# MLP gelu as one ScalarE activation from PSUM, and its second layernorm on VectorE

## The chip, the cores and the metric

The kernel runs on one core of a Trainium2 chip. Its engines are TensorE (PE, with its weight loads shown apart as PEld), VectorE (DVE), ScalarE (ACT), GpSimd (POOL) and SyncE (SP), which here issues the DMAs. The metric is the device time of one execution in microseconds, and of several runs the median.

## What is computed

Two layers, an attention (A) and a gated MLP (B), each run twice over a sequence of 2048 positions with 512 features:

```python
def _gelu(x):
    return jax.nn.gelu(x, approximate=True)

def _layernorm(x, axis=-1, eps=1e-05):
    m = jnp.mean(x, axis=axis, keepdims=True)
    v = jnp.var(x, axis=axis, keepdims=True)
    return (x - m) / jnp.sqrt(v + eps)

def _B_ref(x, w_in, w_sp, b_sp, w_out):
    z = _gelu(jnp.einsum('bsd,df->bsf', x, w_in))
    z1 = z[..., :Fh].copy()
    z2 = _layernorm(z[..., Fh:], axis=-1)
    g = jnp.einsum('ts,bsf->btf', w_sp, z2) + b_sp[None, :, None]
    return jnp.einsum('bsf,fd->bsd', z1 * g, w_out)

x = x + _A_ref(_layernorm(x, axis=-1), A_wq, A_wk, A_wv, A_wo)
x = x + _B_ref(_layernorm(x, axis=-1), B_w_in, B_w_sp, B_b_sp, B_w_out)
x = x + _A_ref(_layernorm(x, axis=-1), A_wq, A_wk, A_wv, A_wo)
x = x + _B_ref(_layernorm(x, axis=-1), B_w_in, B_w_sp, B_b_sp, B_w_out)
```

The attention has 32 query heads of 16 features and one key and value head. In the MLP w_in has 512 x 1792 values and Fh is 896.

## The kernel before

Every operation is put on its engine's program by `K.op(engine, function, waits, inc)`. An engine runs its program in the order in which it was written, and each operation waits for the semaphores in its list. So the order of the calls in the Python is the order on each engine, and only the semaphores tie engines together.

**Prologue.** SP issues the loads of x, of the attention's weights (semaphore `wA`) and of w_in and w_out (semaphore `wB`, lines 212 and 213). VectorE then spreads the attention's weights into padded tiles (L225 to L239), multiplies w_out by 0.5 (L243, which waits for `wB`), and sets up the value tile V_aug (two memsets; the last one is `w_prep`, for which PE and the loads of w_sp wait). Behind these on VectorE stand the statistics of the first layernorm (L277, L278).

**Layer A.** Scores by TensorE (L756), the exponential on ScalarE from PSUM into bf16 (L775), the product with the values by TensorE (L795), and its sum on VectorE (L816 to L820), in a pipeline that runs over 4 query chunks, 8 head groups and 16 key tiles. Side tasks, among them the projection of the queries, the output projection (L717) and in layer 0 the transposes of w_sp, are slipped in between.

**Layer B, gelu stage.** After a layernorm with transposes (L277 to L311) come 60 items: first 32 "z2" items (16 row tiles by 2 halves of 448 columns, matmuls at L904), then 28 "z1" items (4 column chunks by 7 feature tiles, 512 columns, matmuls at L909). Each item is four accumulating matmuls into one of four PSUM banks (`NSLOT = 4`). The gelu of an item is made of five steps:

- `step_pe`: the four matmuls; waits until step d4 of the item four before has freed the bank.
- `step_a0` (L942, ScalarE): a scaled square of the PSUM tile into `ybuf` (fp32).
- `step_d3` (L951, VectorE): (square + c) times the PSUM tile, in `ybuf`.
- `step_a1` (L962, ScalarE): tanh of `ybuf` into `thbuf` (bf16).
- `step_d4` (L972, VectorE): (tanh + 1) times the PSUM tile, into `z2n` or `z1c` (bf16). This is twice the gelu. The factor is made up for by the 0.5 in w_out, and by 4 times the epsilon in the second layernorm.

A loop over the items staggers the steps (`LAG`, one item apart each). A z2 item also has its statistics on VectorE (`bn_stats` L977, and for a whole tile `bn_aggr` L980), then 1/sqrt on GpSimd (L981, L983). Six items later `emit_norm` puts the second layernorm: minus mean over deviation on VectorE (L992, one column), then scale and bias of the 896-wide tile on ScalarE, in place (L995).

**Layer B, behind it.** The spatial matmul (L1060) of 16 matmuls for each of 4 chunks by 7 feature tiles. Its first group waits for the end of the gelu stage and, matmul by matmul, for each tile's norm (`vz2n`). VectorE adds the bias and multiplies by z1 (L1070, L1076), and the output projection follows (L1092, with `w_out_r`), added to X at L1098.

Of the kernel before, what the change touches and what calls it, by code (L numbers as in the profile page):

```python
# [104 lines left out]
def bass_interleave_layers__grouped_kv_mqa__mixer_gmlp__prompt_kernel(  # L105
# [52 lines left out]
    def bank32(b, n=1):  # L158
        return ps32[:, 512 * b:512 * (b + n)]
# [35 lines left out]
    with ExitStack() as wst:  # L195
# [23 lines left out]
        def dve_memset(ap, val, waits=()):  # L219
# [20 lines left out]
                wv_rep[:].rearrange("p kd (g r) -> p kd g r", r=32)[:, :, :, 0:DH],  # L240
                wv_nat[:, :, None, :].to_broadcast([P, KD, 4, DH])),
            waits=[(S_dve, v0), wA], inc=S_dve)
        K.op("dve", lambda e: e.tensor_scalar(w_out_r[:], w_out_r[:], 0.5, None, op0=ALU.mult),  # L243
             waits=[wB], inc=S_dve)
        v0 = dve_memset(V_aug[:], 0.0)
        w_prep_v = dve_memset(V_aug[:].rearrange("p t (c r) -> p t c r", r=32)[:, :, :, DH], 1.0,
                              waits=[(S_dve, v0)])
# [615 lines left out]
    def layer_B(layer_idx, x_waits):  # L863
# [12 lines left out]
        z2n = K.sb([P, NT, FH], BF16, lst, name="z2n")  # L876
        z1c = K.sb([P, NF1, S], BF16, lst, name="z1c")
        NSLOT = 4
        ybuf = K.sb([P, NSLOT, 512], FP32, lst, name="ybuf")
        thbuf = K.sb([P, NSLOT, 512], BF16, lst, name="thbuf")  # L880
        st2 = K.sb([P, NT, 2, 6], FP32, lst, name="st2")
        mv2 = K.sb([P, NT, 2], FP32, lst, name="mv2")
        veps2 = K.sb([P, NT], FP32, lst, name="veps2")
        rstd2 = K.sb([P, NT], FP32, lst, name="rstd2")
        nb2 = K.sb([P, NT], FP32, lst, name="nb2")

        items = []
        for t in range(NT):
# [28 lines left out]
            _, tc, ft = it  # L917
            return z1c[:, ft, tc * TCW:(tc + 1) * TCW]

        st = {"pe": [None] * NIT, "a0": [None] * NIT, "d3": [None] * NIT, "a1": [None] * NIT, "d4": [None] * NIT}  # L920
        vm = [None] * NT

        def step_pe(k):
            it = items[k]
            slot = k % NSLOT
            bk = bank32(slot)
            wl = [xnT_all, wB]
            if k >= NSLOT:
                assert st["d4"][k - NSLOT] is not None
                wl.append((S_dve, st["d4"][k - NSLOT]))  # L930
            st["pe"][k] = K.op("pe", lambda e, it=it, bk=bk: pe_item(e, it, bk), waits=wl, inc=S_pe)

        def step_a0(k):
            it = items[k]
            slot = k % NSLOT
            bk = bank32(slot)
            n = item_N(it)
            wl = [(S_pe, st["pe"][k])]
            if k >= NSLOT:
                wl.append((S_dve, st["d3"][k - NSLOT]))  # L940
                wl.append((S_act, st["a1"][k - NSLOT]))
            st["a0"][k] = K.op("act", lambda e, slot=slot, bk=bk, n=n: e.activation(  # L942
                ybuf[:, slot, 0:n], bk[:, 0:n], ACTF.Square, scale=SQA), waits=wl, inc=S_act)

        def step_d3(k):
            it = items[k]
            slot = k % NSLOT
            bk = bank32(slot)
            n = item_N(it)
            wl = [(S_act, st["a0"][k])]  # L950
            st["d3"][k] = K.op("dve", lambda e, slot=slot, bk=bk, n=n: e.scalar_tensor_tensor(  # L951
                ybuf[:, slot, 0:n], ybuf[:, slot, 0:n], GELU_C, bk[:, 0:n], op0=ALU.add, op1=ALU.mult),
                waits=wl, inc=S_dve)

        def step_a1(k):
            it = items[k]
            slot = k % NSLOT
            n = item_N(it)
            wl = [(S_dve, st["d3"][k])]
            if k >= NSLOT:  # L960
                wl.append((S_dve, st["d4"][k - NSLOT]))
            st["a1"][k] = K.op("act", lambda e, slot=slot, n=n: e.activation(  # L962
                thbuf[:, slot, 0:n], ybuf[:, slot, 0:n], ACTF.Tanh), waits=wl, inc=S_act)

        def step_d4(k):
            it = items[k]
            slot = k % NSLOT
            bk = bank32(slot)
            n = item_N(it)
            wl = [(S_act, st["a1"][k])]  # L970
            oap = out_ap(it)
            st["d4"][k] = K.op("dve", lambda e, slot=slot, bk=bk, n=n, oap=oap: e.scalar_tensor_tensor(  # L972
                oap, thbuf[:, slot, 0:n], 1.0, bk[:, 0:n], op0=ALU.add, op1=ALU.mult),
                waits=wl, inc=S_dve)
            if it[0] == "z2":
                _, t, h = it
                v1 = K.op("dve", lambda e, t=t, h=h: e.bn_stats(st2[:, t, h, :], z2n[:, t, h * 448:(h + 1) * 448]),  # L977
                          waits=[(S_dve, st["d4"][k])], inc=(S_dloc if h == 1 else None))
                if h == 1:
                    vm[t] = K.op("dve", lambda e, t=t: e.bn_aggr(mv2[:, t, :], st2[:, t, :, :]), waits=[(S_dloc, v1)], inc=S_dve)  # L980
                    vp1 = K.op("pool", lambda e, t=t: e.tensor_scalar(veps2[:, t:t + 1], mv2[:, t, 1:2], 4.0 * LN_EPS, None,  # L981
                                                                       op0=ALU.add), waits=[(S_dve, vm[t])], inc=S_ploc)
                    vr2[t] = K.op("pool", lambda e, t=t: e.tensor_tensor(rstd2[:, t:t + 1], veps2[:, t:t + 1], mhalf[:, 0:1], ALU.pow),  # L983
                                  waits=[(S_ploc, vp1)], inc=S_pool)
                    pending_norm.append((k + 6, t))
# [3 lines left out]
        pending_norm = []  # L989

        def emit_norm(t):
            vnb = K.op("dve", lambda e, t=t: e.scalar_tensor_tensor(nb2[:, t:t + 1], mv2[:, t, 0:1], -1.0, rstd2[:, t:t + 1],  # L992
                                                                  op0=ALU.mult, op1=ALU.mult),
                       waits=[(S_pool, vr2[t])], inc=S_dve)
            vz2n[t] = K.op("act", lambda e, t=t: e.activation(z2n[:, t, :], z2n[:, t, :], ACTF.Identity,  # L995
                                                              bias=nb2[:, t:t + 1], scale=rstd2[:, t:t + 1]),
                            waits=[(S_dve, vnb)], inc=S_act)

        LAG = [0, 1, 2, 3, 4]
        for it_k in range(NIT + 5):  # L1000
            k = it_k
            while pending_norm and pending_norm[0][0] <= k:
                emit_norm(pending_norm.pop(0)[1])
            if 0 <= k - LAG[4] < NIT:
                step_d4(k - LAG[4])
            if 0 <= k - LAG[3] < NIT:
                step_a1(k - LAG[3])
            if 0 <= k - LAG[2] < NIT:
                step_d3(k - LAG[2])
            if 0 <= k - LAG[1] < NIT:  # L1010
                step_a0(k - LAG[1])
            if k - LAG[0] < NIT and k - LAG[0] >= 0:
                step_pe(k - LAG[0])
        gelu_done = (S_dve, st["d4"][NIT - 1])
        z1_ready = gelu_done

        while pending_norm:
            emit_norm(pending_norm.pop(0)[1])
        z2n_all = (S_act, max(vz2n))

        wspT = K.sb([P, 2, NT, TCW], BF16, lst, name="wspT")
        hT2 = K.sb([P, NF1, TCW], BF16, lst, name="hT2")
# [13 lines left out]
        for tc in range(NTC):  # L1036
# [9 lines left out]
            for ft in range(NF1):  # L1046
                gb = ft % 3
                bk = bank32(2 + gb)
                wl = [z2n_all, wspT_ready, gelu_done]
                if g_bank_free[gb] is not None:  # L1050
                    wl.append((S_dve, g_bank_free[gb]))

                first_g = (tc == 0 and ft == 0)

                def pe_g(e, ft=ft, bk=bk, wb=wb, first_g=first_g):
                    ins = None
                    for sti in range(NT):
                        if first_g:
                            e.wait_ge(S_act.h, vz2n[sti])
                        ins = e.matmul(bk[:, 0:TCW], z2n[:, sti, ft * 128:(ft + 1) * 128], wspT[:, wb, sti, :],  # L1060
                                       start=(sti == 0), stop=(sti == NT - 1))
                    return ins
                if first_g:
                    wl = [w_ for w_ in wl if w_ is not z2n_all]
                    K.waited["pe"][id(S_act)] = max(K.waited["pe"].get(id(S_act), 0), vz2n[NT - 1])
                vg = K.op("pe", pe_g, waits=wl, inc=S_pe)
                if ft == NF1 - 1:
                    wspT_free[wb] = vg
                wl = [(S_pe, vg), v_bsp_w]
                v1 = K.op("dve", lambda e, gb=gb, bk=bk, tc=tc: e.tensor_tensor(  # L1070
                    gtmp[:, gb, :], bk[:, 0:TCW], bsp_bc[:, tc * TCW:(tc + 1) * TCW], ALU.add),
                    waits=wl, inc=S_dloc)
                wl = [(S_dloc, v1), z1_ready]
                if ft == 0 and hT2_free is not None:
                    wl.append((S_pe, hT2_free))
                vh[ft] = K.op("dve", lambda e, gb=gb, ft=ft, tc=tc: e.tensor_tensor(  # L1076
                    hT2[:, ft, :], gtmp[:, gb, :], z1c[:, ft, tc * TCW:(tc + 1) * TCW], ALU.mult),
                    waits=wl, inc=S_dve)
                g_bank_free[gb] = vh[ft]

            for tt in range(NTT):
                t = tc * NTT + tt
                yb = tt % 2
                bk = bank32(6 + yb)
                wl = [(S_dve, vh[NF1 - 1]), w_prep]
                if y_bank_free[yb] is not None:
                    wl.append((S_dve, y_bank_free[yb]))

# [60 lines left out]
```

## Time and profile before

| | |
|---|---|
| median of 3 runs | 2634.82 us (2631.36 to 2640.33) |
| span of the profiled execution | 2633.1 us, between the fastest run and the median; its own time is not listed apart from its span |
| ScalarE busy | 2066.9 us, 78% of the span |
| TensorE busy | 1897.9 us, 72% |
| VectorE busy | 1225.5 us, 47% |
| GpSimd busy | 43.9 us, 2% |

How to read it: the shares are averages over stages of different kind. The two attentions, from 54 to 1070 us and from 1362 to 2371 us, make up most of the span. The two gelu stages follow at 1104 and 2404 us. In the rows quoted below "idle before" is the time in which the engine stood just ahead of the instructions of a row, with what ended it. In a table of stretches the columns behind each stretch are its length, then the busy time and number of instructions of PE, PEld, DVE, ACT and POOL, the granted TensorE clock as a share of full speed, the DMA's busy share and its GB/s.

### The profile page before, as it was taken

How to read it: one execution, taken by the hardware profiler on the slowest of the kernel's cores; microseconds unless marked ns; L12 is line 12 of the kernel's file. 1: busy time of each engine (PE TensorE's matmuls, PEld its weight loads, DVE VectorE, ACT ScalarE, POOL GpSimd, SP SyncE). 2: the span in 40 equal slices, each digit the busy share in tenths (PEclk: the TensorE clock that was granted, in tenths of full speed). 3: DMA queues.
4: the chain of work that ended last, by engine and by line, in shares of the span. 5: the costliest groups of instructions: out<-in, count | busy, mean ns of one | idle time of the engine just before them, and what ended most of it. 6: DMA issues, size and time to landing. Idle time of an engine off the chain costs nothing.

```text
span 2633.1 us, 29515 instructions
## 1 busy us (share of the span) xinstructions
PE 1897.9 (72%) x11173; PEld 538.9 (20%) x11232; DVE 1225.5 (47%) x2059; ACT 2066.9 (78%) x1639; POOL 43.9 (2%) x95
## 2 busy tenths in 40 slices
PE   2878777777777777468958777777777777764799
PEld 1223111111111111213422111111111111112244
DVE  5565433343334333695366434333433343337933
ACT  1999999999999999181029999999999999973800
POOL 0000000000000000110000000000000000001100
PEclk9996555555555555589979655555655555556899
DMA  3035000000000000201000000000000000001020
GB/s 114 1 88 153 1 1 1 1 1 1 1 1 1 1 1 1 64 1 32 32 1 1 0 1 1 0 1 0 1 1 1 1 0 1 1 1 64 0 68 29
DMA packets 60092, 44.00 MB, mean 17 GB/s; under 512 B 34865, under 2 KB 57265, under 8 KB 59953
## 3 DMA queue, kind: packets, MB, share of 16 engines
q1 hardware_dynamic: 59952, 42.11, 5.4%
q8 instruction: 92, 1.51, 0.2%
q14 instruction: 48, 0.39, 0.0%
HBM read 31.62 MB, written 10.49 MB: 16 GB/s over the span
## 4 chain that ended last, share of the span: by engine, by line
PE 43%; DVE 27%; ACT 20%; issue 8%; POOL 1%; DMA 0%; SPq 0%; another core or an unknown queue 0%; ACTq 0%
PE ps_all L795 20%; ACT P_ring L775 20%; DVE acc_sb L818 13%; PE ps_all L1060 7%; PE ps_all L756 7%; DVE ybuf L951 2%; PE ps_all L1092 2%; PE ps_all L717 2%; DVE ln_stats L277 1%; DVE z2n L972 1%; DVE oT_bf L820 1%; DVE z1c L972 1%; PE ps_all L665 1%; DVE acc_sb L816 1%; PE ps_all L489 1%
## 5 line engine op out<-in xcount | busy, mean ns | idle before, releaser
L775 ACT ACTIVATE P_ring<-ps_all 128x1536 bf16<-128x1536 f32 (+1 forms) x1366 | 1909.5, 1452 | 296.2 <-PE ps_all L756 264.0
L818 DVE TENSOR_TENSOR acc_sb<-ps_all,acc_sb 128x512 f32<-128x512 f32 x896 | 618.1, 690 | 911.2 <-PE ps_all L795 909.8
L795 PE MATMUL ps_all<-P_ring,V_aug 128*32 128x512 bf16 x4096 | 595.9, 569 | 466.8 <-ACT P_ring L775 262.8
L756 PE MATMUL ps_all<-qT_pad,kT_rep 32*128 32x512 bf16 x4096 | 777.7, 568 | 27.1 <-ACT P_ring L775 13.4
L795 PEld LDWEIGHTS ps_all<-P_ring,V_aug 128*32 128x32 bf16 x4096 | 128.6, 100 | 928.3 <-ACT P_ring L775 889.5
L756 PEld LDWEIGHTS ps_all<-qT_pad,kT_rep 32*128 32x128 bf16 x4096 | 141.0, 97 | 580.6 <-issue 416.1
L1060 PE MATMUL ps_all<-wspT,z2n 128*128 128x512 bf16 x878 | 196.8, 383 | 7.7 <-issue 6.8
L942 ACT ACTIVATE ybuf<-ps_all 128x448 f32<-128x448 f32 (+1 forms) x120 | 66.0, 550 | 106.6 <-PE ps_all L904 106.6
L1060 PEld LDWEIGHTS ps_all<-wspT,z2n 128*128 128x128 bf16 x896 | 88.2, 99 | 115.3 <-issue 11.8
L904 PE MATMUL ps_all<-w_in_r,xnTB 128*128 128x448 bf16 x256 | 73.0, 424 | 40.3 <-DVE z2n L972 38.1
L1070 DVE TENSOR_TENSOR gtmp<-ps_all,bsp_bc 128x512 f32<-128x512 f32 x56 | 38.7, 691 | 124.8 <-PE ps_all L1060 124.8
L951 DVE SCALAR_TENSOR_TENSOR ybuf<-ybuf,ps_all 128x448 f32<-128x448 f32 (+1 forms) x120 | 75.3, 628 | 6.4 <-ACT ybuf L942 6.4
L820 DVE TENSOR_TENSOR oT_bf<-ps_all,acc_sb 128x512 bf16<-128x512 f32 x64 | 44.2, 690 | 69.7 <-PE ps_all L795 69.5
L962 ACT ACTIVATE thbuf<-ybuf 128x448 bf16<-128x448 f32 (+1 forms) x120 | 71.2, 594 | 6.7 <-DVE ybuf L951 3.2
L909 PE MATMUL ps_all<-xnTB,w_in_r 128*128 128x512 bf16 x218 | 59.3, 394 | 16.1 <-DVE z1c L972 11.2
L489 PE MATMUL ps_all<-xnTA,wq_pad 128*128 128x512 bf16 x224 | 62.0, 397 | 4.3 <-issue 1.7
L494 DVE CAST qT_pad<-ps_all 128x512 bf16<-128x512 f32 x60 | 41.5, 691 | 50.0 <-PE ps_all L489 50.0
L665 PE MATMUL ps_all<-ident,oT_bf 128*128 128x128 bf16 x256 | 37.2, 296 | 20.2 <-DVE oT_bf L820 20.2
L303 PE MATMUL ps_all<-ident,xnB 128*128 128x128 bf16 x128 | 15.1, 312 | 49.8 <-DVE xnB L292 49.8
L717 PE MATMUL ps_all<-wo_r,onT 128*128 128x512 bf16 x120 | 40.6, 469 | 13.0 <-DVE X L722 6.6
L816 DVE COPY acc_sb<-ps_all 128x512 f32<-128x512 f32 x64 | 43.7, 682 | 9.3 <-PE ps_all L795 9.1
L277 DVE BATCH_NORM_STATS2 ln_stats<-X 128x6 f32<-128x512 bf16 x64 | 42.5, 664 | 0.2
(72 smaller groups left out, 752.2 us busy)
## 6 DMA issues: line engine op xcount, KB each, us to landing
wspT<-wspt_scratch SPq DMA_DIRECT2D x8, 2048.0 KB, 8.3
wsp_stage_21<-in_B_w_sp_dram SPq DMA_DIRECT2D x16, 512.0 KB, 3.9
wspt_scratch<-wspT_tile SPq DMA_DIRECT2D x16, 512.0 KB, 5.0
X<-in_A_x_dram SPq DMA_DIRECT2D x4, 512.0 KB, 5.7
out_dram<-X SPq DMA_DIRECT2D x16, 128.0 KB, 2.9
w_in_r<-in_B_w_in_dram SPq DMA_DIRECT2D x1, 1792.0 KB, 9.6
w_out_r<-in_B_w_out_dram SPq DMA_DIRECT2D x1, 896.0 KB, 10.8
wq_nat<-in_A_wq_dram SPq DMA_DIRECT2D x1, 512.0 KB, 8.0
```

The lines of the kernel that those rows point to most:

```text
L489: ins = e.matmul(side_bank32[:, 0:QC], wq_pad[:, kd, hg, :], xnT[:, kd, qc * QC:(qc + 1) * QC], start=(kd == 0), stop=(kd == KD - 1))
L717: ins = e.matmul(side_bank32[:, 0:D], onT[:, par, c, qt * 128:(qt + 1) * 128], wo_r[:, c, :], start=(c == 0), stop=(c == 3))
L756: ins = e.matmul(bk[:, 0:QC], kT_rep[32 * j:32 * j + 32, kt * 128:(kt + 1) * 128], qT_pad[32 * j:32 * j + 32, hg, qc * QC:(qc + 1) * QC], ...
L775: return e.activation(P_ring[:, s0:s0 + n, :], bank32(b0, n).rearrange("p (k q) -> p k q", k=n)[:, :, 0:QC], ACTF.Exp, scale=DH ** -0.5)
L795: ins = e.matmul(pv_bank[32 * j:32 * j + 32, 0:QC], V_aug[:, kt, 32 * j:32 * j + 32], P_ring[:, slot, :], tile_position=(0, 32 * j), start ...
L816: fn = lambda e: e.tensor_copy(acc_sb[:], pv_bank[:, 0:QC])
L818: fn = lambda e: e.tensor_tensor(acc_sb[:], pv_bank[:, 0:QC], acc_sb[:], ALU.add)
L820: fn = lambda e: e.tensor_tensor(oT_bf[:, par, :], pv_bank[:, 0:QC], acc_sb[:], ALU.add)
L904: ins = e.matmul(bk[:, 0:448], xnT[:, kd, t * 128:(t + 1) * 128], w_in_r[:, kd, FH + h * 448:FH + (h + 1) * 448], start=(kd == 0), stop=(k ...
L951: st["d3"][k] = K.op("dve", lambda e, slot=slot, bk=bk, n=n: e.scalar_tensor_tensor(ybuf[:, slot, 0:n], ybuf[:, slot, 0:n], GELU_C, bk[:, ...
L962: st["a1"][k] = K.op("act", lambda e, slot=slot, n=n: e.activation(thbuf[:, slot, 0:n], ybuf[:, slot, 0:n], ACTF.Tanh), waits=wl, inc=S_act)
L1060: ins = e.matmul(bk[:, 0:TCW], z2n[:, sti, ft * 128:(ft + 1) * 128], wspT[:, wb, sti, :], start=(sti == 0), stop=(sti == NT - 1))
```

## The change

The gelu is computed by one ScalarE activation (`Gelu_apprx_tanh`) that reads the PSUM tile and writes the bf16 result. The steps d3, a1 and d4 go, and with them `ybuf`, `thbuf` and the lags. A PSUM bank is now freed by ScalarE. The result is the gelu itself, so the halving of w_out in the prologue goes and the epsilon is no longer multiplied by 4. The second layernorm is applied by one VectorE instruction with two column scalars, in place of the ScalarE one with its bias column. The waits on these results move with them: `gelu_done` is ScalarE's, `vz2n` is VectorE's, and the output projection waits for `wB` itself.

```diff
-        K.op("dve", lambda e: e.tensor_scalar(w_out_r[:], w_out_r[:], 0.5, None, op0=ALU.mult),
-             waits=[wB], inc=S_dve)
...
             if k >= NSLOT:
-                assert st["d4"][k - NSLOT] is not None
-                wl.append((S_dve, st["d4"][k - NSLOT]))
+                wl.append((S_act, st["a0"][k - NSLOT]))
...
+        def step_gelu(k):
             it = items[k]
             slot = k % NSLOT
             bk = bank32(slot)
             n = item_N(it)
             oap = out_ap(it)
+            st["a0"][k] = K.op("act", lambda e, bk=bk, n=n, oap=oap: e.activation(
+                oap, bk[:, 0:n], ACTF.Gelu_apprx_tanh), waits=[(S_pe, st["pe"][k])], inc=S_act)
             if it[0] == "z2":
                 _, t, h = it
                 v1 = K.op("dve", lambda e, t=t, h=h: e.bn_stats(st2[:, t, h, :], z2n[:, t, h * 448:(h + 1) * 448]),
-                          waits=[(S_dve, st["d4"][k])], inc=(S_dloc if h == 1 else None))
+                          waits=[(S_act, st["a0"][k])], inc=(S_dloc if h == 1 else None))
...
         def emit_norm(t):
-            vnb = K.op("dve", lambda e, t=t: e.scalar_tensor_tensor(nb2[:, t:t + 1], mv2[:, t, 0:1], -1.0, rstd2[:, t:t + 1],
-                                                                  op0=ALU.mult, op1=ALU.mult),
-                       waits=[(S_pool, vr2[t])], inc=S_dve)
-            vz2n[t] = K.op("act", lambda e, t=t: e.activation(z2n[:, t, :], z2n[:, t, :], ACTF.Identity,
-                                                              bias=nb2[:, t:t + 1], scale=rstd2[:, t:t + 1]),
-                            waits=[(S_dve, vnb)], inc=S_act)
-
-        LAG = [0, 1, 2, 3, 4]
...
+            vz2n[t] = K.op("dve", lambda e, t=t: e.tensor_scalar(z2n[:, t, :], z2n[:, t, :], mv2[:, t, 0:1], rstd2[:, t:t + 1],
+                                                                op0=ALU.subtract, op1=ALU.mult),
+                           waits=[(S_pool, vr2[t]), (S_dve, vm[t])], inc=S_dve)
+
+        for k in range(NIT + 2):
             while pending_norm and pending_norm[0][0] <= k:
                 emit_norm(pending_norm.pop(0)[1])
...
+            if k < NIT:
+                step_pe(k)
+            if 0 <= k - 1 < NIT:
+                step_gelu(k - 1)
+        gelu_done = (S_act, st["a0"][NIT - 1])
...
-        z2n_all = (S_act, max(vz2n))
+        z2n_all = (S_dve, max(vz2n))
...
-                            e.wait_ge(S_act.h, vz2n[sti])
+                            e.wait_ge(S_dve.h, vz2n[sti])
...
-                wl = [(S_dve, vh[NF1 - 1]), w_prep]
+                wl = [(S_dve, vh[NF1 - 1]), w_prep, wB]
```

More of the change, by code (lines that the diff above doesn't have):

```diff
@@ L878, in layer_B @@
         NSLOT = 4
-        ybuf = K.sb([P, NSLOT, 512], FP32, lst, name="ybuf")
-        thbuf = K.sb([P, NSLOT, 512], BF16, lst, name="thbuf")
         st2 = K.sb([P, NT, 2, 6], FP32, lst, name="st2")
@@ L884, in layer_B @@
         rstd2 = K.sb([P, NT], FP32, lst, name="rstd2")
-        nb2 = K.sb([P, NT], FP32, lst, name="nb2")
         items = []
@@ L918, in out_ap @@
             return z1c[:, ft, tc * TCW:(tc + 1) * TCW]
-        st = {"pe": [None] * NIT, "a0": [None] * NIT, "d3": [None] * NIT, "a1": [None] * NIT, "d4": [None] * NIT}
+        st = {"pe": [None] * NIT, "a0": [None] * NIT}
         vm = [None] * NT
@@ L928, in step_pe @@
             if k >= NSLOT:
-                assert st["d4"][k - NSLOT] is not None
-                wl.append((S_dve, st["d4"][k - NSLOT]))
+                wl.append((S_act, st["a0"][k - NSLOT]))
             st["pe"][k] = K.op("pe", lambda e, it=it, bk=bk: pe_item(e, it, bk), waits=wl, inc=S_pe)
-        def step_a0(k):
+        def step_gelu(k):
             it = items[k]
@@ L937, in step_a0 @@
             n = item_N(it)
[L938 to L970, printed above, removed]
             oap = out_ap(it)
-            st["d4"][k] = K.op("dve", lambda e, slot=slot, bk=bk, n=n, oap=oap: e.scalar_tensor_tensor(
-                oap, thbuf[:, slot, 0:n], 1.0, bk[:, 0:n], op0=ALU.add, op1=ALU.mult),
-                waits=wl, inc=S_dve)
+            st["a0"][k] = K.op("act", lambda e, bk=bk, n=n, oap=oap: e.activation(
+                oap, bk[:, 0:n], ACTF.Gelu_apprx_tanh), waits=[(S_pe, st["pe"][k])], inc=S_act)
             if it[0] == "z2":
@@ L977, in step_d4 @@
                 v1 = K.op("dve", lambda e, t=t, h=h: e.bn_stats(st2[:, t, h, :], z2n[:, t, h * 448:(h + 1) * 448]),
-                          waits=[(S_dve, st["d4"][k])], inc=(S_dloc if h == 1 else None))
+                          waits=[(S_act, st["a0"][k])], inc=(S_dloc if h == 1 else None))
                 if h == 1:
                     vm[t] = K.op("dve", lambda e, t=t: e.bn_aggr(mv2[:, t, :], st2[:, t, :, :]), waits=[(S_dloc, v1)], inc=S_dve)
-                    vp1 = K.op("pool", lambda e, t=t: e.tensor_scalar(veps2[:, t:t + 1], mv2[:, t, 1:2], 4.0 * LN_EPS, None,
+                    vp1 = K.op("pool", lambda e, t=t: e.tensor_scalar(veps2[:, t:t + 1], mv2[:, t, 1:2], LN_EPS, None,
                                                                        op0=ALU.add), waits=[(S_dve, vm[t])], inc=S_ploc)
@@ L991, in emit_norm @@
         def emit_norm(t):
-            vnb = K.op("dve", lambda e, t=t: e.scalar_tensor_tensor(nb2[:, t:t + 1], mv2[:, t, 0:1], -1.0, rstd2[:, t:t + 1],
-                                                                  op0=ALU.mult, op1=ALU.mult),
-                       waits=[(S_pool, vr2[t])], inc=S_dve)
-            vz2n[t] = K.op("act", lambda e, t=t: e.activation(z2n[:, t, :], z2n[:, t, :], ACTF.Identity,
-                                                              bias=nb2[:, t:t + 1], scale=rstd2[:, t:t + 1]),
-                            waits=[(S_dve, vnb)], inc=S_act)
-        LAG = [0, 1, 2, 3, 4]
-        for it_k in range(NIT + 5):
-            k = it_k
+            vz2n[t] = K.op("dve", lambda e, t=t: e.tensor_scalar(z2n[:, t, :], z2n[:, t, :], mv2[:, t, 0:1], rstd2[:, t:t + 1],
+                                                                op0=ALU.subtract, op1=ALU.mult),
+                           waits=[(S_pool, vr2[t]), (S_dve, vm[t])], inc=S_dve)
+        for k in range(NIT + 2):
             while pending_norm and pending_norm[0][0] <= k:
                 emit_norm(pending_norm.pop(0)[1])
[L1004 to L1014, printed above, removed]
+            if k < NIT:
[3 more added lines that the diff above has]
+        gelu_done = (S_act, st["a0"][NIT - 1])
         z1_ready = gelu_done
@@ L1064, in layer_B @@
                     wl = [w_ for w_ in wl if w_ is not z2n_all]
-                    K.waited["pe"][id(S_act)] = max(K.waited["pe"].get(id(S_act), 0), vz2n[NT - 1])
+                    K.waited["pe"][id(S_dve)] = max(K.waited["pe"].get(id(S_dve), 0), vz2n[NT - 1])
                 vg = K.op("pe", pe_g, waits=wl, inc=S_pe)
```

## The prediction

> **What bounds the kernel now.** I read the page first, for the span and the chain of waits, then the busy time of each engine by stretches, which cuts the span into stages.
>
> ```profile
> span 2633.1 us, 29515 instructions
> PE 43%; DVE 27%; ACT 20%; issue 8%; POOL 1%; DMA 0%; SPq 0%; another core or an unknown queue 0%; ACTq 0%
> ...
> 54.00:1070.00 1016.00, 752.16 (x4815) 192.71 (x4830) 433.61 (x674) 952.90 (x683) 0.00 (x0) 0.59 0.06 16
> 1070.00:1104.00 34.00, 8.41 (x67) 6.91 (x68) 24.02 (x57) 0.00 (x0) 5.06 (x8) 0.50 0.39 124
> 1104.00:1154.00 50.00, 32.84 (x115) 10.33 (x113) 46.41 (x102) 37.48 (x66) 9.50 (x24) 0.82 0.00 0
> 1154.00:1197.00 43.00, 31.32 (x121) 9.58 (x124) 42.09 (x79) 38.94 (x69) 3.17 (x8) 1.00 0.00 1
> 1197.00:1330.00 133.00, 122.81 (x549) 54.72 (x560) 52.42 (x77) 1.60 (x3) 0.00 (x0) 0.99 0.10 32
> ```
>
> After the times of a stretch come the busy times of PE, PEld, DVE, ACT and POOL, then the granted TensorE clock. Attention (54 to 1070, and again in the second half) is ScalarE's: 953 of 1016 us. The change does not touch it. The MLP's gelu stage, 1104 to 1197, is VectorE's: 46.4 of 50 and 42.1 of 43 us. Behind it the spatial matmul is PE's, 122.8 of 133 us. So the change works in the one stage of a layer where the engine it relieves is the bound. The chain of waits shows both edges of the stage (the L972 row is the timeline's).
>
> ```profile
> 1103.14 3.18 PE ps_all L904 x8
> ...
> 1195.65 1.04 PE ps_all L909 x4
> 1196.69 3.38 issue
> 1198.51 1.46 DVE L972 SCALAR_TENSOR_TENSOR z1c<-thbuf,ps_all 128x512 bf16<-128x512 bf16 x2
> 1200.07 10.03 PE ps_all L1060 x38
> ...
> 2404.24 3.18 PE ps_all L904 x8
> ...
> 2501.17 9.72 PE ps_all L1060 x38
> ```
>
> From the first L904 matmul to the first of L1060 are 1200.07 - 1103.14 = **96.9 us**, and 2501.17 - 2404.24 = 96.9 in the second MLP. The "issue" piece of 3.38 us is the drain of the five-deep lag: L1060 waits for the last L972, which ends at 1199.97.
>
> **The removed work.** The groups by form give the stage's operations (engine, shape, count in both layers, busy us, mean ns):
>
> ```profile
> L951 DVE SCALAR_TENSOR_TENSOR ybuf<-ybuf,ps_all 128x448 f32<-128x448 f32 x64 | 37.5, 587 | 6.4 <-ACT ybuf L942 6.4
> L972 DVE SCALAR_TENSOR_TENSOR z2n<-thbuf,ps_all 128x448 bf16<-128x448 bf16 x64 | 39.2, 613 | 0.0
> L977 DVE BATCH_NORM_STATS2 st_38<-z2n 128x6 f32<-128x448 bf16 x32 | 20.1, 627 | 1.1
> L980 DVE BATCH_NORM_AGGREGATE mv_39<-st_38 128x2 f32<-128x12 f32 x16 | 3.3, 208 | 0.6
> L942 ACT ACTIVATE ybuf<-ps_all 128x448 f32<-128x448 f32 x64 | 33.6, 526 | 106.6 <-PE ps_all L904 106.6
> L942 ACT ACTIVATE ybuf<-ps_all 128x512 f32<-128x512 f32 x56 | 32.4, 579 | 0.0
> L995 ACT ACTIVATE z2n<-z2n,nb_42,rstd_41 128x896 bf16<-128x896 bf16 x16 | 18.1, 1132 | 11.7 <-DVE nb_42 L992 11.6
> L775 ACT ACTIVATE P_ring<-ps_all 128x1536 bf16<-128x1536 f32 x1364 | 1907.6, 1452 | 296.2 <-PE ps_all L756 264.0
> L775 ACT ACTIVATE P_ring<-ps_all 128x1024 bf16<-128x1024 f32 x2 | 2.0, 1018 | 0.0
> L775 ACT ACT_TABLE_LOAD x1 | 1.3, 1283 | 0.7 <-PEq L1134 0.7
> L292 DVE TENSOR_SCALAR xnB<-X,ln_mv,ln_rstd 128x512 bf16<-128x512 bf16 x32 | 11.0, 408 | 11.8 <-POOL ln_rstd L284 11.8
> L243 DVE TENSOR_SCALAR w_out_r<-w_out_r 128x3584 bf16<-128x3584 bf16 x1 | 1.1, 1093 | 5.3 <-DMA w_out_r<-in_B_w_out_dram 5.3
> ```
>
> L951, L962 (the tanh) and L972 go in all 60 items of a layer, L992 and L995 in all 16 tiles, and the square (L942) becomes the gelu. What remains per item is four matmuls, one ScalarE pass and, on the 32 z2 items, half a tile of statistics.
>
> **The new gelu on ScalarE** has no row. The exp rows, PSUM to bf16 as the gelu will be, give (1452 - 1018) / 512 = 0.85 ns an element and 150 ns fixed: 0.53 us for 448, 0.58 for 512. The square (L942) reads the same PSUM tiles in 526 and 579 ns. As bounds I keep 0.53 and, at twice the slope, 0.91 and 1.02. I take 0.53 and 0.58, where both functions agree.
>
> **The norm on VectorE** (896 wide, bf16, pointer scalars): between 0.41 (L292, 512 wide) and 1.25 (two L977). The line from L292 to L243 gives 408 + 384 x 685 / 3072 = 0.49 us. VectorE then has 2 x 0.627 + 0.208 + 0.49 = 1.95 us a tile, 31 us for 16 tiles, at most 2.7 us a tile and 43 us. That is hidden, since PSUM is freed by ScalarE alone and the stage lasts longer than either (next step). Its cover is gone above 50 / 16 = 3.1 us a tile. The statistics now wait for ScalarE, and behind them on VectorE stand the norms, for which L1060's first group waits. They end some 15 us before it. Cost: nothing. SBUF addresses that shift: nothing.
>
> **What is late next: PE.** Its slot is freed one ScalarE pass after the matmul, and with four slots it runs ahead. Its pace is the granted clock's:
>
> ```profile
> 1103.00:1107.00 4.00, 3.86 (x11) 1.64 (x12) 0.78 (x3) 1.19 (x3) 0.00 (x0) 0.50 0.00 0
> 1111.00:1121.00 10.00, 4.70 (x21) 1.60 (x22) 9.72 (x23) 7.46 (x13) 2.19 (x6) 1.00 0.00 1
> 1121.00:1131.00 10.00, 7.76 (x24) 2.17 (x24) 9.72 (x22) 8.17 (x15) 2.36 (x6) 0.66 0.00 0
> 1170.00:1197.00 27.00, 22.53 (x86) 6.80 (x88) 27.00 (x46) 25.33 (x47) 0.00 (x0) 1.00 0.00 0
> ...
> 1107.60 0.15 PEld L904 LDWEIGHTS ps_all<-w_in_r,xnTB 128*128 128x128 bf16 x1 [0.22 <-issue]
> 1107.94 1.04 PEld L904 LDWEIGHTS ps_all<-w_in_r,xnTB 128*128 128x128 bf16 x6 [0.19 <-issue]
> 1109.85 0.93 PE L904 MATMUL ps_all<-w_in_r,xnTB 128*128 128x448 bf16 x4 [0.42 <-DVE z2n L972]
> ...
> 1244.21 10.74 PE ps_all L1060 x49
> ...
> 1200.45 0.15 PEld L1060 LDWEIGHTS ps_all<-wspT,z2n 128*128 128x128 bf16 x1 [0.28 <-issue]
> 1203.44 2.49 PEld L1060 LDWEIGHTS ps_all<-wspT,z2n 128*128 128x128 bf16 x12 [0.28 <-issue]
> ```
>
> At clock 0.5 the loads come every 0.15 + 0.22 = 0.37 us, until 1107.94, 4.8 us into the stage: 13 matmuls. At full clock four take 0.93 with a last one of 0.37, so (0.93 - 0.37) / 3 = 0.187 each. For 512 columns the 49 in a row give 10.74 / 49 = 0.219. L1060 runs dense at 0.99, and L909 at 1.00 with PE busy for 22.5 of 27 us, so I take full clock after the start:
> 4.8 + 115 x 0.187 + 112 x 0.219 = 4.8 + 21.5 + 24.5 = 50.8 us.
> An item takes 0.75 to 0.88 us, above ScalarE's 0.53 to 0.58, so PE is the bound. At the end come the last matmul's 0.2, the gelu's 0.58 and some 0.1 of hand-over: **51.7 us**. That saves 96.9 - 51.7 = 45.2 us a layer. L1060 now opens at half clock, seven loads 0.43 apart from 1200.45 to 1203.44 and one before; with the 3.38 us gap shrunk to 0.9 this should go, 8 x (0.43 - 0.219) = 1.7 us. Per layer 46.9, for two 93.8 us.
>
> **The w_out scaling.** The timeline of the prologue:
>
> ```profile
> 14.83 0.23 DVE L239 COPY wv_rep<-wv_nat 128x256 bf16<-128x256 bf16 x1
> 20.37 1.09 DVE L243 TENSOR_SCALAR w_out_r<-w_out_r 128x3584 bf16<-128x3584 bf16 x1 [5.32 <-DMA w_out_r<-in_B_w_out_dram]
> 21.62 0.91 DVE L220 MEMSET V_aug<- 128x1024 uint32 x1 [0.16 <-issue]
> 22.64 0.64 DVE L277 BATCH_NORM_STATS2 ln_stats<-X 128x6 f32<-128x512 bf16 x1
> ```
>
> VectorE stands for 5.32 us on a DMA whose data nothing else needs before the first MLP, with the layernorm of all of layer 0 queued behind. Without L243 the memset starts at 15.1: 21.62 - 15.1 = **6.5 us**, straight on the path. The wsp loads that SP issues behind w_prep go out as much earlier, beside the tail of w_out and b_sp; their transposes are background tasks behind the q tasks, so nobody waits. PE's new waits for wB (L1092) are met over 1000 us before.
>
> **The table.** The whole program has one ACT_TABLE_LOAD, 1.28 us, at 0.72 us, far ahead of the first exp at 52.8. If gelu needs another table, ScalarE loads at three switches: exp to gelu twice, gelu to exp once. ScalarE is idle before each (no row in 1070 to 1104), and the one load seen did not wait for its matmul. Taken: nothing. Bounds: 0 and 3 x 1.28 = 3.8 us.
>
> **Sum.** 93.8 + 6.5 = 100.3 us off the profiled span of 2633.1: 2532.8. The median of the runs is 2634.82, 1.7 more than that span, which I take as what lies around it: **2534.5 us**.
>
> **The rivals.**
> Loads exposed at all three switches: 2534.5 + 3.8 = 2538.3. For it: the next layer's exp or gelu could stand behind its load after the wait. Against: the place of the one load, and for the gelus PE's four slots, 6 us deep at half clock. Chance 0.12. The Trainium skill (ScalarE: Activation LUTs, What ACT_TABLE_LOAD costs) speaks against the change here: each switch of set costs 1283 ns and a drain of 1380, 2.66 us. By it an estimate of the sum is 8.0 us less gain, 2542.5; the 1283 agrees with the row, the drain stands in no row here.
> The clock oscillates, as in 1121 to 1131 at 0.66: (128 x 0.187 + 112 x 0.219) / 0.66 + 0.9 = 74 us a layer, saving 23: 2634.8 - 46 - 6.5 = 2582. For it: attention's clock is 0.59 with PE busy for 752 of 1016 us. Against: dense 128-row matmuls hold 0.99 in L1060. Chance 0.06. The Trainium skill (TensorE: Matmul & The Clock Gate, A second HAM failure mode: psum-queue depth-cycling) holds that cycling PSUM banks with small idle gaps makes the clock swing; four banks cycle here, but L909 cycles them at 1.00, so I give it little.
> The clock stays at 0.5: 128 x 0.37 + 112 x 0.43 + 0.9 = 96.4 us, so only the prologue and 1 us go: 2627, no measurable change. Chance 0.03.
> Gelu at twice the exp's slope: ScalarE is the bound, 32 x 0.91 + 28 x 1.02 = 57.7 and 1.5 to fill; saving 96.9 - 59.2 + 1.7 = 39.4 a layer: 2550. Chance 0.04.
> The other side: a table load ahead of each of the 60 gelus. An item then takes 1.28 + 0.53 or 0.58, so 32 x 1.81 + 28 x 1.86 + 1.5 = 111.5 us: 14.6 lost a layer, less 6.5 gained, 2657.5. It decides against the change from a ScalarE item of about 1.65 us. Against: 1366 exps share one load. Chance 0.03.
>
> **The numbers.** The forecast has 0.72. Its own range, 2526 to 2542, comes from the runs' spread (2631.36 to 2640.33) and the half-clock start, 2.4 us a layer if absent. Up to 2554 the range takes in the exposed loads and the slower gelu: 0.88 together. A measurement tells 0.3%, 8 us, from no change: faster 0.94, same 0.03, slower 0.03.
>
> **What would show it.** Right: L904's first matmul to L1060's first about 52 us, PE busy in nearly all of it at a clock near 0.95, gelu rows of 0.53 and 0.58 us, the first ln_stats at 16 us, four table loads in idle stretches. Wrong: PE waiting for ScalarE in the stage, a clock under 0.9 there, more than four table loads, or L1060 waiting for the norms.

## The result, and the profile after

The changed kernel takes 2535.72 us (median of 4 runs, 2530.56 to 2538.38), the kernel before 2633.33 (4 runs). The ratio is **0.9621**, 95% interval 0.9601 to 0.9640. The forecast was 2534.5 us. The profiled execution took 2537.05 us, its span is 2535.0; so 2.05 us lay around the span, where the forecast had taken 1.7.

The page of the changed kernel gives the new span, and its chain of waits the edges of both gelu stages. L899 and L904 are the old L904 and L909, L1009 is the old L1060:

```profile
span 2535.0 us, 29045 instructions
...
1096.81 26.63 PE ps_all L899 x128
1123.50 10.74 PE ps_all L904 x49
...
1147.62 0.73 issue
1148.35 8.36 PE ps_all L1009 x38
...
2352.92 26.63 PE ps_all L899 x128
...
2404.46 8.36 PE ps_all L1009 x38
```

Each stage lasts 1148.35 - 1096.81 = 2404.46 - 2352.92 = **51.54 us**, instead of 96.93. In the old chain VectorE held the stage almost from end to end. In its first half (z2) L951 and L972 alternated with the statistics L977, in its second (z1) with each other, every 0.60 us:

```profile
1108.74 0.52 DVE ybuf L951
1109.26 0.54 DVE z2n L972
1109.80 0.02 issue
1109.83 0.64 DVE st_38 L977
...
1184.83 0.60 DVE ybuf L951
1185.43 0.60 DVE z1c L972
```

Now the chain runs through the stage on PE alone: one piece of 128 matmuls, then the 512-column ones at the dense pace of 10.74 us for 49. The gap ahead of the spatial matmul, 3.38 us before, is 0.73. PE is the bound, and the busy times by stretches say the same:

```profile
1063.00:1097.00 34.00, 8.31 (x67) 6.63 (x66) 24.08 (x57) 0.00 (x0) 5.06 (x8) 0.50 0.38 124
1097.00:1148.30 51.30, 50.46 (x237) 23.93 (x238) 27.14 (x64) 34.12 (x61) 14.95 (x32) 0.96 0.00 1
...
1097.00:1101.00 4.00, 4.00 (x12) 1.61 (x11) 1.03 (x2) 1.09 (x2) 0.00 (x0) 0.50 0.01 2
1101.00:1105.00 4.00, 4.00 (x22) 2.02 (x21) 3.02 (x7) 2.61 (x5) 1.61 (x4) 0.95 0.00 0
1105.00:1123.00 18.00, 18.00 (x97) 9.32 (x96) 17.62 (x44) 12.87 (x25) 10.09 (x22) 1.00 0.00 1
```

PE is busy for 50.5 of 51.3 us. The clock is 0.50 in the first 4 us, as before, and then stays at 1.00, where it had swung between 0.66 and 1.00. VectorE is still nearly full from 1105 to 1123 (17.6 of 18 us), but nobody waits for it there. The groups by form of the new operations, and the timeline of ScalarE at its table loads and of VectorE at the head of the program:

```profile
L933 ACT ACTIVATE z2n<-ps_all 128x448 bf16<-128x448 f32 x64 | 34.8, 543 | 117.6 <-PE ps_all L899 117.6
L933 ACT ACTIVATE z1c<-ps_all 128x512 bf16<-128x512 f32 x56 | 33.4, 597 | 15.0 <-PE ps_all L904 15.0
L952 DVE TENSOR_SCALAR z2n<-z2n,mv_57,rstd_59 128x896 bf16<-128x896 bf16 x16 | 7.5, 476 | 0.5 <-POOL rstd_59 L943 0.5
...
1046.56 1.28 ACT L933 ACT_TABLE_LOAD   x1
1098.52 0.54 ACT L933 ACTIVATE z2n<-ps_all 128x448 bf16<-128x448 f32 x1 [50.68 <-PE ps_all L899]
1148.27 1.28 ACT L773 ACT_TABLE_LOAD   x1
...
14.52 0.23 DVE L239 COPY wv_rep<-wv_nat 128x256 bf16<-128x256 bf16 x1
14.91 0.91 DVE L220 MEMSET V_aug<- 128x1024 uint32 x1 [0.16 <-issue]
15.93 0.64 DVE L275 BATCH_NORM_STATS2 ln_stats<-X 128x6 f32<-128x512 bf16 x1
```

Gelu does need another table: four loads in all (two for L773, two for L933). One stands at the start of the program. Each of the other three is issued as soon as the last instruction on the old table is through, not behind the matmul that its own activation waits for: the one at 1046.56 ends 50.7 us ahead of the first gelu.

Where the 98.1 us of span went, each figure a difference of starts in the two traces:

| part of the span | after less before, us |
|---|---|
| to the first ln_stats (22.64 before, 15.93 after) | **-6.7** |
| from there to the first gelu matmul | +0.4 |
| first gelu stage | **-45.4** |
| first spatial stage, up to the next ln_stats (1330.27 before, 1276.89 after) | -1.7 |
| from there through the second attention to the second gelu matmul | +2.1 |
| second gelu stage | **-45.4** |
| the rest | -1.4 |

### The profile page after: what moved, and what is told of

It reads as the page before. It is cut to its first block, busy times and chain, and to the rows that moved or that the text cites. A ratio compares the mean times of both kernels' runs of the same rounds, so it can differ in the third digit from the quotient of the medians.

```text
span 2535.0 us, 29045 instructions
## 1 busy us (share of the span) xinstructions
PE 1869.0 (74%) x11173; PEld 548.9 (22%) x11232; DVE 1096.2 (43%) x1818; ACT 1984.8 (78%) x1490; POOL 48.5 (2%) x95
## 4 chain that ended last, share of the span: by engine, by line
PE 48%; DVE 21%; ACT 21%; issue 8%; POOL 1%; DMA 0%; SPq 0%; another core or an unknown queue 0%; ACTq 0%; DVEq 0%
PE ps_all L793 21%; ACT P_ring L773 21%; DVE acc_sb L816 14%; PE ps_all L1009 8%; PE ps_all L754 7%; PE ps_all L899 2%; PE ps_all L1041 2%; PE ps_all L904 2%; PE ps_all L715 2%; DVE ln_stats L275 2%; DVE oT_bf L818 1%; PE ps_all L663 1%; DVE acc_sb L814 1%; PE ps_all L301 1%; PE ps_all L487 1%
## 5 line engine op out<-in xcount | busy, mean ns | idle before, releaser
L773 ACT ACTIVATE P_ring<-ps_all 128x1536 bf16<-128x1536 f32 (+1 forms) x1366 | 1911.4, 1452 | 286.2 <-PE ps_all L754 255.1
L1009 PE MATMUL ps_all<-wspT,z2n 128*128 128x512 bf16 x878 | 193.7, 379 | 2.4 <-issue 1.5
L933 ACT ACTIVATE z2n<-ps_all 128x448 bf16<-128x448 f32 x64 | 34.8, 543 | 117.6 <-PE ps_all L899 117.6
L1009 PEld LDWEIGHTS ps_all<-wspT,z2n 128*128 128x128 bf16 x896 | 87.5, 98 | 107.7 <-issue 2.4
L899 PE MATMUL ps_all<-w_in_r,xnTB 128*128 128x448 bf16 x256 | 53.3, 374 | 1.6 <-DVE xnTB L309 1.6
L904 PE MATMUL ps_all<-xnTB,w_in_r 128*128 128x512 bf16 x218 | 48.0, 379 | 0.3
L933 ACT ACTIVATE z1c<-ps_all 128x512 bf16<-128x512 f32 x56 | 33.4, 597 | 15.0 <-PE ps_all L904 15.0
```

Source lines behind the costliest of these rows:

```text
L773: return e.activation(P_ring[:, s0:s0 + n, :], bank32(b0, n).rearrange("p (k q) -> p k q", k=n)[:, :, 0:QC], ACTF.Exp, scale=DH ** -0.5)
L899: ins = e.matmul(bk[:, 0:448], xnT[:, kd, t * 128:(t + 1) * 128], w_in_r[:, kd, FH + h * 448:FH + (h + 1) * 448], start=(kd == 0), stop=(k ...
L904: ins = e.matmul(bk[:, 0:TCW], w_in_r[:, kd, ft * 128:(ft + 1) * 128], xnT[:, kd, tc * TCW:(tc + 1) * TCW], start=(kd == 0), stop=(kd == K ...
```

## The experiments

The theory on trial: the single gelu hands the stage from VectorE to PE, the norm costs nothing on VectorE, the prologue's stand is a gain of its own, and the table costs nothing. The rivals: the norm's move off ScalarE is the real gain, the table loads cost, or the clock or VectorE is a bound in hiding.

**1. The prologue alone.** In the changed kernel:

```diff
+        K.op("dve", lambda e: e.tensor_scalar(w_out_r[:], w_out_r[:], 1.0, None, op0=ALU.mult),
+             waits=[wB], inc=S_dve)
         v0 = dve_memset(V_aug[:], 0.0)
```

> The changed kernel with the scaling of w_out put back in the prologue, with a factor of 1.0 that changes no value. My theory, that VectorE's stand for w_out's DMA lies straight on the path: first ln_stats back from 15.9 to about 22.6 us, time 6.7 us above the changed kernel, 2542; gelu stages unchanged at 51.5 us. Rival, that the attention behind it takes the shift up (its pipeline settles against ScalarE anyway): within 2 us of 2536.

Measured: 2542.18 us, ratio 0.9646 (0.9630 to 0.9662). The timeline has the old stand back:

```profile
20.11 1.09 DVE L243 TENSOR_SCALAR w_out_r<-w_out_r 128x3584 bf16<-128x3584 bf16 x1 [5.32 <-DMA w_out_r<-in_B_w_out_dram]
...
22.39 0.64 DVE L277 BATCH_NORM_STATS2 ln_stats<-X 128x6 f32<-128x512 bf16 x1
```

The first ln_stats stands 22.39 - 15.93 = 6.5 us later, and the median is 2542.18 - 2535.72 = 6.5 us higher. The intervals of the two ratios overlap a little, so the times alone don't settle it; with the stand in the trace they do. The stages are unchanged (1156.59 - 1104.97 = 51.6).

**2. The norm back on ScalarE.** In the changed kernel `emit_norm` gets its old pair of operations back:

```diff
-            vz2n[t] = K.op("dve", lambda e, t=t: e.tensor_scalar(z2n[:, t, :], z2n[:, t, :], ...
+            vnb = K.op("dve", lambda e, t=t: e.scalar_tensor_tensor(nb2[:, t:t + 1], mv2[:, t, 0:1], -1.0, ...
+            vz2n[t] = K.op("act", lambda e, t=t: e.activation(z2n[:, t, :], z2n[:, t, :], ACTF.Identity, ...
```

> The changed kernel with the second layernorm applied on ScalarE again (the removed pair of operations). My theory: a z2 tile then costs ScalarE 2 x 0.54 + 1.13 = 2.2 us, above PE's 1.51, so ScalarE sets the z2 half: 16 x 2.2 = 35 us, then 24.5 us of z1 at PE's pace; stage 60 to 62 us, time 2536 + 2 x 9.5 = 2555. Rival, that four PSUM banks and the lag of six items hide the norm on either engine: stage 52 us, 2536. Rival, that the norm's move is half of the whole gain: stage above 70 us, 2573 or more.

Measured: 2576.24 us, ratio 0.9778 (0.9764 to 0.9793); the stage lasts 72.6 us (1093.60 to 1166.16). That is the third line of the expectation, not my theory: of the 45.4 us that a stage gains, 72.56 - 51.54 = 21.0 are lost again without the norm's move. But in the stretch of the z2 half ScalarE is busy for only 34.9 of 55 us, and VectorE for 23.1, so neither is at its limit. The chain of waits, two tiles of it:

```profile
1119.49 1.17 DVE st L938 x2
1120.66 0.02 issue
1120.68 0.21 DVE mv L941
1120.89 0.03 DVE nb L953
1120.92 0.02 issue
1120.95 1.14 ACT z2n L956
1122.08 0.44 ACT z2n L934
1122.52 0.02 issue
1122.54 1.17 DVE st L938 x2
```

It is a ring: the norm on ScalarE waits for its bias column `nb`; the column stands on VectorE behind the newest tile's statistics; these wait for that tile's gelus, which stand on ScalarE behind the norm before. Each tile goes once around: 1122.54 - 1119.49 = 3.05 us. I formed a second theory, that the order in the queues makes this and not the place of the norm, and made run 3.

**3. The norm on ScalarE, its column made earlier.** As run 2, but VectorE is given `nb` three items ahead of ScalarE's norm (the column one item earlier than in run 2, the norm two items later):

```diff
-                    pending_norm.append((k + 6, t))
+                    pending_nb.append((k + 5, t))
+                    pending_norm.append((k + 8, t))
```

> The norm on ScalarE as in the earlier run of that kind, but its bias column is made on VectorE three items ahead of the ScalarE instruction instead of right before it. If the 73 us of that stage are a ring (ScalarE's norm waits for the column, the column stands on VectorE behind the newest tile's statistics, these wait for ScalarE's gelu: 1.14 + 0.44 + 1.17 + 0.21 + 0.04 + hand-overs = 3.06 us a tile), the ring is open now and ScalarE's own work sets the z2 half: about 2.15 x 16 = 34.4 us, stage 60 to 62, time 2555. If not the ring but the norm on ScalarE itself costs it: stage 73 us, 2576 as before.

Measured: 2540.48 us, ratio 0.9642 (0.9626 to 0.9659); stage 1146.01 - 1090.24 = 55.77 us. The ring is gone, and with it 16.8 of the 21.0 us that run 2 had lost in a stage. ScalarE is the bound now, with a tile in 1.87 us:

```profile
1109.64 1.05 ACT L934 ACTIVATE z2n<-ps_all 128x448 bf16<-128x448 f32 x2
1110.49 1.22 ACT L962 ACTIVATE z2n<-z2n,nb,rstd 128x896 bf16<-128x896 bf16 x1
1111.51 1.06 ACT L934 ACTIVATE z2n<-ps_all 128x448 bf16<-128x448 f32 x2
```

I had expected 2.15 a tile and a stage of 60 us or more: I had added up durations, but back to back these instructions overlap. So the place of the norm is worth 55.77 - 51.54 = 4.2 us a stage, and the other 16.8 belong to the ring, which the change opens as well, since the norm on VectorE needs no bias column and holds up no gelu. The 4.2 rest on the traces: the medians differ by 4.8 us where the two stages together give about 8, and the intervals of the ratios overlap.

**4. The norm's move without the new gelu.** In the kernel before, only `emit_norm` is changed, to the VectorE form of the change, and `vz2n` is VectorE's.

> The kernel before with only the second layernorm moved to VectorE (the gelu stays in four steps). My theory, that VectorE is the bound of that stage: it loses 0.15 us a tile (the bias column) and gains 0.48, 0.33 x 16 = 5.2 us a layer: stage 102 us, time 2633 + 10.5 = 2644, slower than before. Rival, that ScalarE's 1.13 us in the middle of its queue held the lag of the steps: stage below 96.9 us, faster than 2633.

Measured: 2642.25 us, ratio 1.0029 (1.0017 to 1.0041): slower by 0.3%, as my theory had it. The chain of waits has the spatial matmul's first piece at 1202.77, and the first gelu matmul is at 1100.45: a stage of 102.3 us instead of 96.9, for 102 expected. The norm's move costs 5.4 us a stage where VectorE is the bound. Where it is not, it saves 4.2 (against run 3) or 21.0 (against run 2).

**5. A table load in every item.** In the changed kernel every second item gives exp instead of gelu:

```diff
-                oap, bk[:, 0:n], ACTF.Gelu_apprx_tanh), waits=[(S_pe, st["pe"][k])], inc=S_act)
+                oap, bk[:, 0:n], ACTF.Gelu_apprx_tanh if k % 2 == 0 else ACTF.Exp), waits=...
```

> The changed kernel with the exponential in place of the gelu in every second item, so that ScalarE must change its table 60 times in a stage (those items give exp, not gelu). It prices a load on the path. By the row (1.283 us, nothing beside it): items of 1.28 + 0.54 and 0.60, 32 x 1.83 + 28 x 1.88 = 111 us a stage, time 2536 + 2 x 60 = 2656. By the Trainium skill's figure (ScalarE: Activation LUTs, What ACT_TABLE_LOAD costs: a drain of 1.38 us beside each load) an estimate is 32 x 3.2 + 28 x 3.26 = 194 us a stage, 2821. If both functions were in one table: no more than four loads, 2536.

Measured: 2664.85 us in its one run, the kernel before 2634.97; the stage is 1209.20 - 1095.91 = 113.3 us. ScalarE's timeline:

```profile
1129.72 1.28 ACT L933 ACT_TABLE_LOAD   x1
1131.01 0.54 ACT L933 ACTIVATE z2n<-ps_all 128x448 bf16<-128x448 f32 x1
1131.57 1.28 ACT L933 ACT_TABLE_LOAD   x1
```

An item takes 1131.57 - 1129.72 = 1.85 us: the load, 0.01, the activation, 0.02. This is the rival of the forecast that ends slower than before, put into a kernel, and its price was right: 113.3 us against the 111.5 given there. It also weighs the page: the Trainium skill (ScalarE: Activation LUTs, What ACT_TABLE_LOAD costs) puts a drain of 1.38 us beside each load, by which an estimate of the stage was 194 us. No such time stands in these rows; the measurement decides. The four loads of the changed kernel would cost at most 1.3 us each, and they fall into idle time.

**6. The half clock at the head of the stage.** In the changed kernel:

```diff
             if c == NCH - 1:
+                def pe_warm(e):
+                    for i in range(16):
+                        ins = e.matmul(bank32(5)[:, 0:448], xnT[:, i % KD, 0:128], w_in_r[:, i % KD, 0:448], start=True, stop=True)
+                    return ins
+                K.op("pe", pe_warm, waits=[(S_dve, vlast), wB], inc=S_pe)
```

> The changed kernel with 16 matmuls of 448 columns, whose results nobody reads, ahead of the fourth chunk's transposes in each MLP, where PE is idle. If the first 4.8 us of the gelu stage run at half clock because PE was idle before, and 6 us of matmuls bring the clock up: 13 x 0.187 = 2.4 us less a stage, stage 49.1 us, time 2531. If the gap of about 2 us behind them drops the clock again, or the clock follows something else: stage 51.5 us, 2536. If the extra matmuls delay the transposes: stage 51.5, the layernorm longer by what they overlap, at most 1 us.

Measured: 2528.20 us, ratio 0.9597 (0.9576 to 0.9618). The chain of waits:

```profile
1084.22 6.12 PE ps_all L875 x16
1092.18 24.39 PE ps_all L907 x128
...
1141.47 24.35 PE ps_all L1017 x112
```

The stage is 49.3 us for 49.1 expected; its first 128 matmuls take 24.39 instead of 26.63. So the head runs at half clock because PE had little to do ahead of it (8.3 of 34 us), and 6 us of matmuls lift it. They were just enough: 16 in 6.12 us are 0.38 each, half pace to the end. The Trainium skill (TensorE: Matmul & The Clock Gate, Part 1: The HAM clock gate) has the clock rise after about 3.4 us of sustained work; here the half clock lasted some 4.5 us at the head of the changed kernel's stages, 6 us in this run's extra matmuls, and 2.9 us in those of run 10's first layer. In this execution the first gelu matmul also stands 4.6 us earlier than in the changed kernel's, though only an idle PE ahead of it was given work: the first attention, which the edit leaves alone, took 4.8 us less. It differs by that much from one execution to another (see the part on why the prediction was right), and the intervals overlap, so I claim only the 2.2 us a stage.

**7 and 8. How much VectorE work is hidden.** Each statistics instruction of a z2 half is done twice, or three times (the additional results are not read):

```diff
+                for x in range(2):
+                    K.op("dve", lambda e, t=t, h=h, x=x: e.bn_stats(st2x[:, x, t, h, :], z2n[:, t, h * 448:(h + 1) * 448]),
+                         waits=[(S_act, st["a0"][k])], inc=S_dloc)
                 v1 = K.op("dve", lambda e, t=t, h=h: e.bn_stats(st2[:, t, h, :], ...
```

> The changed kernel with every bn_stats of a z2 half done twice (the second result is not read): 2 x 0.6 us more for VectorE in a tile, 1.7 + 1.2 = 2.9 us a tile, 46 us in all. My theory, that VectorE is hidden up to 3.1 us a tile: norms end 3 to 4 us ahead of L1009's counterpart, stage 51.5 us, time unchanged within 2 us. Rival, that VectorE's pace already reaches PE through the waits: stage longer by up to 19 us.

> The changed kernel with every bn_stats of a z2 half done three times: 1.7 + 2.4 = 4.1 us a tile, 65.6 us for 16 tiles, 2 us to start. My theory: the cover is gone, the spatial matmul's first group waits tile by tile for the norms and the stage plus that wait ends about 16 x 4.1 + 2 = 67 us behind the first gelu matmul; the first group can start at 52 us and follows the norms, so its end moves by 14 to 16 us less the 3.4 us that the group takes by itself: 11 to 15 us a layer, time 2558 to 2566. Rival, that VectorE is hidden anyway by the spatial matmul's own lead: unchanged.

Measured, one run each: 2538.01 and 2554.53 us. With two, the last norm starts at 1144.69, ends 4 us ahead of the spatial matmul (1149.28), and the stage is 1149.28 - 1097.70 = 51.6 us: hidden, with a tile every 2.75 us on VectorE. With three the cover is gone, and the timeline shows the spatial matmul's first group, which began at 1145.49, held tile by tile:

```profile
1148.61 0.39 PE L1013 MATMUL ps_all<-wspT,z2n 128*128 128x512 bf16 x1 [0.59 <-DVE z2n L956]
1152.41 0.39 PE L1013 MATMUL ps_all<-wspT,z2n 128*128 128x512 bf16 x1 [3.41 <-DVE z2n L956]
1156.20 1.03 PE L1013 MATMUL ps_all<-wspT,z2n 128*128 128x512 bf16 x2 [3.41 <-DVE z2n L956]
```

A tile takes VectorE 3.8 us instead of the 4.1 expected, since its instructions overlap too, so the loss is a little under the range given. The limit that the forecast named, 3.1 us a tile, lies between the two runs.

**9. Beyond the change: the layernorm beside the gelu.** With VectorE idle for nearly half of the stage (busy for 27.1 of 51.3 us), the layernorm ahead of it, 34 us in which PE is busy for 8, can run beside it. Items are ordered by chunk (8 z2, then 7 z1), a matmul waits for its own chunk's transposes only, and the next chunk's statistics go to VectorE first:

```diff
+        ln_dve(0)
+        ln_T(0)
...
+            if k < NIT and k % PERC == 0 and k // PERC + 1 < NCH:
+                ln_dve(k // PERC + 1)
+            if k < NIT and k % PERC == 2 * CT + 2 and k // PERC + 1 < NCH:
+                ln_T(k // PERC + 1)
```

> A version beyond the change: the layernorm of chunk c+1 on VectorE runs beside the gelu items of chunk c (8 z2 and 7 z1 items for each chunk, transposes in banks 6 and 7). If PE's idle 34 us ahead of the stage can now be filled because VectorE has room, VectorE needs 5.3 + 6.8 + 1.5 = 13.6 us a chunk and PE 12.2 us: from the first statistics to the first spatial matmul 8 + 4 x 13.6 + 1 = 63 us instead of 78 (1069.9 back to 1070.6 us before, 33 + 51.5 = 85), 20 us less a layer, time 2496. If the waits between the three engines or a swinging clock eat it: 2510 to 2536.

Measured: **2491.71 us**, ratio 0.9463 (0.9437 to 0.9490), faster than both kernels. The chain of waits:

```profile
1062.16 0.71 DVE ln_stats L275
...
1124.91 1.24 PE ps_all L1030 x5
```

From the first statistics to the first spatial matmul are 1124.91 - 1062.16 = 62.8 us (63 expected), where the changed kernel takes 1148.35 - 1064.34 = 84.0.

**10. The same with the clock lifted**, by 14 matmuls nobody reads at the head of the layer, as in run 6.

> The overlapped version with 14 matmuls of 448 columns, whose results nobody reads, at the head of each MLP, beside the first chunk's statistics, where PE stands idle for 6.3 us. If the half clock at the head of the stage comes from that idle time: first 32 gelu matmuls 6.1 instead of 8.7 us, first transposes 1.1 instead of 1.9, some 3 us less a layer, time 2486. If the extra matmuls come too late and delay the transposes, or the clock falls again in the 2 us behind them: 2491 or up to 1 us more.

Measured: 2492.37 us, ratio 0.9457 (0.9443 to 0.9472), no gain in the time. The clock did rise: the first 32 matmuls take 6.23 us instead of 8.70. But from the first statistics to the first spatial matmul are still 1124.30 - 1062.16 = 62.1 us, 0.6 less than in run 9. The timeline shows what took the rest:

```profile
1081.58 1.28 DVE L309 COPY xnTB<-ps_all 128x1024 bf16<-128x1024 bf16 x2
1082.92 6.23 PE L913 MATMUL ps_all<-w_in_r,xnTB 128*128 128x448 bf16 x32
1095.94 1.28 DVE L309 COPY xnTB<-ps_all 128x1024 bf16<-128x1024 bf16 x2
1097.28 6.23 PE L913 MATMUL ps_all<-w_in_r,xnTB 128*128 128x448 bf16 x32 [1.20 <-DVE xnTB L309]
```

A chunk takes 1097.28 - 1082.92 = 14.4 us, and PE waits 1.2 at its end for VectorE's copies of the transposes, which come 1095.94 - 1081.58 = 14.4 us apart (13.6 a chunk was expected of VectorE). VectorE's queue (statistics, norms, copies, and in each chunk a stand of 1.5 us for GpSimd's 1/sqrt) is the bound of the overlapped stage; a faster PE only waits longer. In run 9 the copies are 14.4 us apart too. There PE's slow start let it begin the second chunk 2.4 us after they were done, and at 13 us a chunk it had 0.1 us of this left at the fourth, so it never waited.

## Why the prediction was right, point by point

- **The bound moves from VectorE to PE at full clock.** Forecast 51.7 us a stage, measured 51.54. The sum's parts hold: half clock for the first 4 to 5 us, then 1.00; 0.75 to 0.88 us an item on PE against a gelu of 0.543 and 0.597 (forecast 0.53 and 0.58).
- **The drain and the opening of the spatial matmul.** The gap went from 3.38 to 0.73 us (0.9 expected), and with it the half clock at the opening (38 matmuls in 8.36 us, 10.03 and 9.72 before): -1.7 and -1.4 us for the spatial stages (1.7 expected).
- **The norm is hidden on VectorE.** 0.476 us forecast as 0.49. My 1.95 us a tile was too much: in the changed kernel the tiles follow each other every 1.69 us, since VectorE's instructions overlap when they stand in a row (two statistics take 1.15). The last norm ends at 1129.0, 19 us ahead of the spatial matmul; I had said 15. That the cover reaches to 3.1 us a tile fits runs 7 and 8 (2.75 hidden, 3.8 not).
- **The prologue.** 6.5 forecast, 6.7 in the traces, 6.5 in run 1.
- **The table.** Gelu needs its own, and the loads cost nothing, as taken. The rival of exposed loads is out by their places in the timeline, the one of a load in every item by the count of four, with its price confirmed in run 5.
- **The clock rivals.** A clock that swings with four PSUM banks did not come: the banks cycle at 1.00. The stay at half clock did not come either.
- **What the sum lacked, and luck.** It gives 100.3 us, the spans differ by 98.1. The 2.2 us come from the parts with the attentions (+0.4 and +2.1), which the forecast left as they were. From the program's first ln_stats to that of the first MLP lies the first attention, whose code no edit here touches; it took from 1041.8 to 1050.1 us in the twelve traces of this document (1048.0 before, 1048.4 after). So I count the 2.2 us as spread; whether a part of it is real stays open. By the same spread it is luck that the forecast of the time came within 1.2 us. What holds without luck are the stages.

Where my reasons failed was in the experiments: for run 2 I priced the norm on ScalarE by its duration and missed that its place in two queues closes a ring.

## What to carry to other kernels

Ask which engine is full in the very stage that a change touches, then price the stage anew by the next engine, with the clock that the profile grants it there: that gave a stage of 51.7 us for a measured 51.5. An operation moved between engines is worth what the bound of its stage makes of it (the same norm's move cost 5.4 us a stage in one kernel and saved 4.2 to 21 in the other). In queues that run in order, see to it that an operand is made before the instruction that needs it comes up: where the making itself waits for work that stands behind that instruction, as in run 2, the two queues form a ring, and neither is full.

## What the hardware showed that I had not expected

- ScalarE instructions back to back overlap: two gelus of 0.54 us (the changed kernel's mean) and a norm of 1.14 (run 2), 2.22 together, come every 1.87 us in run 3. VectorE's statistics do too: 0.63 us alone, two in a row 1.15 (changed kernel).
- A table load is not held by the wait of the activation behind it: it was issued at 1046.56, right behind the last exp, for a gelu that started at 1098.52. On the path it cost 1.31 us an item, with 0.01 and 0.02 us around it (run 5).
